# Weight staging, mask, score and ring choices of a planned attention and maxout kernel, five batches split in place of seven

## The chip, the cores and the metric

The kernel runs on one core of a Trainium2 chip. The metric is device time in microseconds of one execution. A core has five engines that run side by side: TensorE (PE: matmuls, with its weight loads shown as PEld), VectorE (DVE), ScalarE (ACT), GpSimd (POOL) and SyncE (SP, which here only issues DMAs and waits for them). Data lie in on-chip memory of 128 partitions; matmuls write to PSUM, a small memory that VectorE and ScalarE read out.

## The reference

Eight batches, eight heads, 576 positions, head size 64. Causal attention with a bias that falls with the running sum of max(s, 0), and then a feed-forward layer whose hidden layer is the largest of three products:

```python
scores = scale * np.matmul(q, k.transpose(0, 1, 3, 2))
cum = np.cumsum(np.maximum(s, 0.0), axis=-1)
bias = -(cum[:, :, :, None] - cum[:, :, None, :])
scores = np.where(causal, -1000000000.0, scores + np.minimum(bias, 0.0))
attn = np.exp(scores - np.max(scores, axis=-1, keepdims=True))
attn = attn / (np.sum(attn, axis=-1, keepdims=True) + 1e-09)
x = np.matmul(attn, v)                      # heads side by side: 4608 x 512
h = np.maximum(np.maximum(x @ w1, x @ w2), x @ w3)   # 768 wide
return h @ w_out
```

All inputs and the output are 32-bit floats, except that the weights arrive as 64-bit floats and are turned on the chip.

## The kernel before

**Splitting numbers.** Most matmuls run in 16 bits: a 32-bit number is kept as a high half and a low half (the rest after rounding), and a product is three matmuls (high by high, high by low, low by high). The scores use 32-bit matmuls: either the raw numbers, or a rounded high part `qh` and a low part `ql` in three terms (`scores_of`, L1125 to L1179). `RAWS` and `RAW0` say which units take raw ones.

**Units.** Two heads share one unit of 128 partitions. `ORDER` lists how batches are worked: `s` (split) does the first 256 rows of queries of a batch, in two units of two head pairs each; `r` (rest) does the other 320 rows of that batch, in four units of one pair; `w` (whole) does both at once, in four units. Before, seven batches are split and one is whole. A unit loads `qr` (q and k), `rv` (v) and `bias` (L744, L753, L857, L868, L880), splits v into `vv` (L808 to L818) and, where scores are not raw, q and k into `qh` and `ql` (L947 to L965). A step of 128 query rows (`one_step`, L1192) is: the causal mask laid over the bias by GpSimd (L1222, for units from `MASKU` on; for units before it TensorE adds a triangle of large negative numbers to the scores, L1159), scores on TensorE (L1149), sum and maximum on VectorE (L1235), exponential on ScalarE (L1244), division into high and low halves (L1280, L1288), a transpose by DMA (L1299), and values on TensorE (L1384, `values`). The last 64 query rows of two units are done together (`both`, L1018). Units 0 and 1 (below `ND`) use 32-bit numbers and TensorE transposes instead (`turned`, L1305).

**Experts.** When all four pairs of a batch's phase (256 or 320 rows) are done, `experts` (L1445) computes the hidden layer, six blocks of three `u` matmul groups (L1479), whose maximum is kept in a tile `m1` (L1494, L1502) and split into halves (L1509 on ScalarE, L1514 on GpSimd, or on VectorE for sets below `EARLYSET`). Then come four `d` groups (L1535), each copied to a tile `o` (L1554) and sent out (L1560). Tiles `m1` come from a ring of three, tiles `o` from a ring of two.

**Weights.** 24 weight blocks (18 for `u`, 6 for the output) are loaded as 64-bit floats (L477), turned into 32-bit floats (`d1` L485 on ScalarE, then either `d2` and `d3` on VectorE, L489 and L493, or `top` on GpSimd, L499, and `join` on VectorE, L506; `LOWP` says for which blocks), scaled per group of three by a bound that TensorE (L527, L434) and VectorE work out, and split into halves (L599, L637). The raw block stays in one of seven places until its halves are made. The first phase of batch 0 does not wait for halves: it uses raw blocks in 32-bit matmuls (`first_set`, L659, L689).

**Bias.** The running sums of all rows are made once (L368 to L399), written to memory and read back for each unit, spread over all partitions. Units below `NPB` do not wait for that: below `NDB` they load their rows of s spread over the partitions and scan them there (L884 to L909); otherwise TensorE spreads the sums with a matmul (L918).

**The order.** Nothing waits in program order by itself. Each operation is handed to a planner (`Plan`) with a cost for each engine that may do it, a key and the tiles that it reads and writes. `Plan.run` (L121) walks through modelled time and lets each free engine take the ready operation with the lowest key; the sequence so found is written out, and every engine then runs its part in that order. So keys (`PACE`, `LOOK`, `FAST`) and costs decide the order of the program, not its work. Operations with a `mode` use TensorE in tiles smaller than its full array; the planner holds one back for a while (`HOLD`, L163) so that several of them go together. DMAs on SP are modelled by `load` (L316):

```python
def load(emit, key, nbytes, reads=(), writes=(), queue="SP", rate=0.3, lat=2000.0, begin=0.0):
    plan.add({queue: (lat, 450.0, nbytes / rate * 1e-3)}, emit, key, reads, writes).ready = begin
```

The functions that the change touches, and what calls them:

## Time and profile before

| | |
|---|---|
| median of three runs | 785.98 us (785.86 to 788.97) |
| the profiled execution | 784.61 us |
| its span, first to last instruction | 782.6 us |
| VectorE, ScalarE, GpSimd busy | 573.8, 519.2, 308.3 us |
| bytes moved by DMA | 136.31 MB |
| `u` matmuls (L1479) | 3240, busy 411.3 us |
| `d` matmuls (L1535) | 1080, busy 137.9 us |

A row of the profile's groups reads: line, engine, operation, written tile <- read tiles, shapes, count | busy us, mean ns of one | idle time of the engine just before them, and what ended most of it. A row of a timeline reads: start us, us, engine, line, operation, tiles, shapes, count, and in brackets the idle time before. A row of waits reads: engine and line <- engine and line waited for: total us, times, longest us. Matmuls overlap each other, so a sum of mean durations is more than the busy time, and the start of one to the start of the next is its price.

### The profile page before, as it was taken

Reading aid. Unit: us, or ns where it says so; the run is one execution under the profiler, and the core shown is the slowest. Engines: PE = TensorE matmul, PEld = TensorE weight load, DVE = VectorE, ACT = ScalarE, POOL = GpSimd, SP = SyncE. Lnnn points to the kernel's source line nnn. Section 1 sums busy time; section 2 is a strip of 40 time slices with the busy share of each in tenths; the row PEclk is TensorE's granted clock in tenths of the full one; section 3 lists DMA queues with packets and bytes.
Section 4 is the critical chain, followed back from the end, with each engine's and each line's share of the span. In section 5 each row is a group of like instructions: output and inputs, shape, how many; then the busy total and the mean of one; then the engine's idle time right before and its main releaser. Section 6 shows DMA issues by size and latency. Waiting matters only on the chain. (4 is left out here: it accounts for less than half of the span.)

```text
span 782.6 us, 19630 instructions
## 1 busy us (share of the span) xinstructions
PE 764.8 (98%) x7189; PEld 589.6 (75%) x7189; DVE 573.8 (73%) x1691; ACT 519.2 (66%) x1369; POOL 308.3 (39%) x361
## 2 busy tenths in 40 slices
PE   7889999999999999999999899999999999999998
PEld 5677888888888877766788677667776777778875
DVE  6999898875587888888878787888787977322131
ACT  6878777871687787986887777777876977111101
POOL 4432423641355455444544364354444452011110
PEclk9999999999999999999999999999999999999999
DMA  9799778890399899998999999898989865300000
GB/s 342 245 260 242 180 169 164 176 237 18 97 207 233 199 175 214 227 215 200 225 232 207 183 192 240 241 190 198 254 210 169 208 137 100 81 1 34 28 2 34
DMA packets 241167, 136.31 MB, mean 174 GB/s; under 512 B 204080, under 2 KB 222000, under 8 KB 241072
## 3 DMA queue, kind: packets, MB, share of 16 engines
q1 hardware_dynamic: 240912, 134.78, 75.7%
q8 instruction: 56, 0.92, 0.5%
q14 instruction: 39, 0.32, 0.2%
q10 hardware_dynamic: 160, 0.30, 0.1%
HBM read 75.64 MB, written 9.58 MB: 109 GB/s over the span
## 5 line engine op out<-in xcount | busy, mean ns | idle before, releaser
L1479 PE MATMUL u<-x,w 128*128 128x320 f16 (+1 forms) x3240 | 411.3, 287 | 2.9 <-ACT o L1554 2.9
L1479 PEld LDWEIGHTS <-w 128*128 128x128 f16 x3240 | 312.6, 98 | 99.5 <-issue 17.6
L1514 POOL TENSOR_TENSOR h<-m,h 128x320 f16<-128x320 f32 (+1 forms) x90 | 69.9, 777 | 190.4 <-ACT h L1509 174.5
L1535 PE MATMUL d<-h,w 128*128 128x320 f16 (+1 forms) x1080 | 137.9, 287 | 0.1
L1502 DVE SCALAR_TENSOR_TENSOR m<-u,m 128x320 f32<-128x320 f32 (+1 forms) x180 | 82.2, 457 | 64.3 <-PE u L1479 60.1
L1535 PEld LDWEIGHTS <-w 128*128 128x128 f16 x1080 | 104.7, 98 | 30.4 <-issue 3.2
L1222 POOL TENSOR_SCALAR_AFFINE_SELECT p<-bias 128x256 f32<-128x256 f32 (+3 forms) x91 | 68.9, 770 | 120.6 <-DVE pr L1288 68.9
L1244 ACT ACTIVATE p<-p,sc 128x256 f32<-128x256 f32 (+3 forms) x182 | 98.2, 540 | 26.3 <-DVE sc L1235 25.6
L1509 ACT ACTIVATE h<-m 128x320 f16<-128x320 f32 (+1 forms) x90 | 39.4, 438 | 102.9 <-DVE m L1502 102.6
L1288 DVE SCALAR_TENSOR_TENSOR pr<-p,sc,pr 128x256 f16<-128x256 f32 (+3 forms) x182 | 100.3, 567 | 8.0 <-ACT pr L1280 7.8
L1280 ACT ACTIVATE pr<-p,sc 128x256 f16<-128x256 f32 (+3 forms) x182 | 89.3, 538 | 13.0 <-DMA pT<-pr 7.9
L961 POOL TENSOR_TENSOR ql<-qr,qh 128x256 fp32r<-128x256 f32 (+1 forms) x76 | 82.5, 1106 | 35.0 <-ACT qh L949 30.6
L1235 DVE CUSTOM_DVE_ANT_0 p<-s,p 128x256 f32<-128x256 f32 (+3 forms) x182 | 80.4, 467 | 3.7 <-POOL p L1222 2.2
L1384 PEld LDWEIGHTS <-vv 128*64 128x64 f16 x1232 | 58.6, 110 | 18.1 <-issue 10.0
L1384 PE MATMUL av<-pT,vv 128*64 128x320 f16 (+3 forms) x1104 | 70.3, 276 | 1.2 <-DVE x L1429 0.8
L1494 DVE TENSOR_SCALAR m<-u 128x320 f32<-128x320 f32 (+1 forms) x55 | 25.3, 461 | 48.2 <-PE u L1479 47.6
L1554 ACT ACTIVATE o<-d,os 128x320 f32<-128x320 f32 (+1 forms) x60 | 28.2, 498 | 47.6 <-PE d L1535 36.8
L766 DVE TENSOR_REDUCE am<-rv 128x1 f32<-128x640 f32 (+1 forms) x44 | 33.9, 777 | 13.2 <-DMA rv<-in_qkv_dram 13.0
L1222 POOL TENSOR_SCALAR_AFFINE_SELECT ha<-bias 128x1024 f32<-128x1024 f32 (+3 forms) x29 | 26.7, 926 | 41.8 <-DVE r L1288 29.8
L1244 ACT ACTIVATE ha<-ha,sc 128x512 f32<-128x512 f32 (+3 forms) x58 | 35.9, 620 | 6.5 <-DVE sc L1235 6.1
L815 DVE SCALAR_TENSOR_TENSOR vv<-rv,vs,vv 128x640 f16<-128x640 f32 (+1 forms) x44 | 39.0, 887 | 0.4
L1288 DVE SCALAR_TENSOR_TENSOR r<-ha,sc,r 128x512 f16<-128x512 f32 (+3 forms) x58 | 37.5, 660 | 2.3 <-ACT r L1280 2.2
(170 smaller groups left out, 980.1 us busy)
## 6 DMA issues: line engine op xcount, KB each, us to landing
bias<-cd SPq DMA_DIRECT2D x32, 576.0 KB, 5.0
qr<-in_qkv_dram SPq DMA_DIRECT2D x28, 480.0 KB, 5.2
rv<-in_qkv_dram SPq DMA_DIRECT2D x32, 320.0 KB, 3.8
raw<-in_w_dram SPq DMA_DIRECT2D x16, 512.0 KB, 5.7
qr<-in_qkv_dram SPq DMA_DIRECT2D x13, 512.0 KB, 6.3
bias<-cd SPq DMA_DIRECT2D x12, 512.0 KB, 5.4
out_dram<-o SPq DMA_DIRECT2D x32, 160.0 KB, 2.4
early<-in_w_dram SPq DMA_DIRECT2D x8, 512.0 KB, 7.0
```

The source lines that it names most:

```text
L961: lambda e, d0=d0, d1=d1: E[e].tensor_tensor(out=lo().bitcast(F32R)[:, d0:d1], in0=raw()[:, d0:d1], in1=hi()[:, d0:d1], op=ALU.subtract),
L1222: nc.gpsimd.affine_select(out=pt()[:, 0:8 * P].rearrange("p (j n) -> p j n", j=2)[:, :, at:at + nk], in_=r["bias"]()[:, 2 * a * w:2 * (a + ...
L1235: lambda e, j=j: nc.vector.tensor_tensor_reduce(out=pj(j), in0=src(j), in1=pj(j) if masked else bias(j), scale=-SCALE, scalar=3.0e38, op0= ...
L1244: lambda e, j=j: nc.scalar.activation(out=pj(j), in_=pj(j), func=AF.Exp, scale=-1.0, bias=nm()[:, j:j + 1], accum_out=sm()[:, j:j + 1]),
L1280: lambda e, h_=h_, s_=s_, j=j: nc.scalar.activation(out=h_(), in_=s_(), func=AF.Copy, scale=ri()[:, j:j + 1]),
L1288: lambda e, h_=h_, l_=l_, s_=s_, j=j: nc.vector.scalar_tensor_tensor(out=l_(), in0=s_(), scalar=ri()[:, j:j + 1], in1=h_(), op0=ALU.mult, ...
L1384: nc.tensor.matmul(av()[j * D:(j + 1) * D, c0:nq], lhsT=lt, rhs=rt, start=(n < 2), stop=(n >= len(todo) - 2), skip_group_check=True,)
L1479: nc.tensor.matmul(pm()[:, :nq], lhsT=v[:, wt, kt, :], rhs=x(xt, kt), start=(k == 0), stop=(k == 3 * NKT - 1),)
L1502: lambda e, pm=pm, m1=m1: nc.vector.scalar_tensor_tensor(out=m1()[:, :nq], in0=pm()[:, :nq], scalar=HSC, in1=m1()[:, :nq], op0=ALU.mult, o ...
L1509: lambda e, m1=m1, ft=ft: nc.scalar.activation(out=h(0, ft), in_=m1()[:, :nq], func=AF.Copy),
L1514: lambda e, m1=m1, ft=ft: E[e].tensor_tensor(out=h(1, ft), in0=m1()[:, :nq], in1=h(0, ft), op=ALU.subtract),
L1535: nc.tensor.matmul(pm()[:, :nq], lhsT=v[:, wt, dt, :], rhs=h(c, ft), start=(k == 0), stop=(k == 3 * NFT - 1), skip_group_check=True,)
```

## The change

It changes constants of the planner and of the kernel, and some functions. In words:

- `ORDER`: batches 0 to 4 are split, 5 to 7 are whole. `RAWS` 10: all split units use raw scores. `MASKU` 4: units 0 to 3 get their mask from TensorE. `NDB` 1: unit 0 scans its own bias. `FUSE0` 2: split units from 2 on compute the values of both pairs in one operation.
- `RAWX`, `RAWAT`: eleven places for raw weight blocks; the four new ones are the two `qh` and two `ql` buffers. `LATE`: the halves get keys later by 10. `PACE`: other weight keys. `LOWP` from 0: blocks 0 and 1 also use GpSimd's `top`.
- Tiles `o` come from the ring of `m1`, now five deep. `EARLYSET` 4: the low halves of expert sets 1 to 3 are made by VectorE. `EARLY` 2: low parts `ql` are always made by GpSimd. `P3` 12: the third set of attention buffers is used from unit 12 on.
- The planner: other rules for grouping operations with a mode, other costs for DMAs (a lead before a transfer occupies the queue, other rates and latencies), for the scale matmul and for the 32-bit transposes; other keys (`LOOK`, `FAST`, `HOLD`).
- New code that its constants leave unused: `far_power` (`FAR` 99), `split_first` (`D16` 0), half PSUM tiles in `first_set` (`KP` 0). The code for the output matmuls moves from `experts` into `down_all` without a change but for the ring and the cost of the load.

```diff
-PACE = (0.9, -1.0, 3000.0)
-EARLY = 8
-EARLYSET = 0
-LOOK = (10.0, 4.0, 5.0, 3.5)
+PACE = (0.5, 3.0, 3000.0)
+EARLY = 2
+EARLYSET = 4
+LOOK = (10.0, 4.0, 2.0, 3.5)
...
-MASKU = 0
+MASKU = 4
...
-FAST = 8
-HOLD = (3000.0, 30000.0)
+FAST = 4
+HOLD = (2000.0, 30000.0, 2)
+SAME = 1
+D16 = 0
+SPARE = 1000.0
+FAR = 99
...
+KP = 0
+HOLD2 = (3000.0, 900.0e3, 2)
...
-NDB = 0
+NDB = 1
...
-RAWS = 6
-FUSE0 = 99
+RAWS = 10
+FUSE0 = 2
...
-P3 = 10
-LOWP = (2, 24)
+P3 = 12
+RAWX = 1
+LATE = 10.0
+LOWP = (0, 24)
...
-ORDER = ('s0', 's1', 's2', 's3', 's4', 's5', 'r0', 'r1', 's6', 'r2', 'r3', 'r4', 'r5', 'r6', 'w7')
+ORDER = ('s0', 's1', 's2', 's3', 's4', 'r0', 'r1', 'r2', 'r3', 'r4', 'w5', 'w6', 'w7')
...
-                    if kept is not None and op.mode:
-                        break
-                    if e == "PE" and op.mode and not shape and op.due > now > HOLD[1]:
-                        kept = op
+                    if e == "PE" and op.mode:
+                        kept.append(op)
+                        if shape and (op.mode == shape or not SAME):
+                            pick = op
+                            break
+                        if not shape and (len(kept) >= (HOLD2 if now > HOLD2[1] else HOLD)[2] or not op.due > now > HOLD[1]):
+                            pick = kept[0]
+                            break
                         continue
-                    pick = op
+                    pick = kept[0] if kept and shape else op
                     break
...
-                    dma[e] = max(dma[e], now + busy) + op.ways[e][2]
+                    dma[e] = max(dma[e], now + op.ways[e][3]) + op.ways[e][2]
...
-        qr=2, qh=2, ql=2, rv=4, vv=2, bias=2, p=2, pr=2, tl=2, pT0=2, pT1=2, tT=2, t=5, m1=3, o=2,
-        sc=6, dg=2, am=3, vs=5, ws=3, os=4, s=2, av=1, m=3,
+        qr=2, qh=2, ql=2, rv=4, vv=2, bias=2, p=2, pr=2, tl=2, pT0=2, pT1=2, tT=2, t=5, m1=5,
+        sc=6, far=1, dg=2, am=3, vs=5, ws=3, os=4, s=2, av=1, m=3,
...
-    def load(emit, key, nbytes, reads=(), writes=(), queue="SP", rate=0.3, lat=2000.0, begin=0.0):
-        plan.add({queue: (lat, 450.0, nbytes / rate * 1e-3)}, emit, key, reads, writes).ready = begin
+    def load(emit, key, nbytes, reads=(), writes=(), queue="SP", rate=0.36, lat=1285.0, begin=0.0, lead=1440.0):
+        plan.add({queue: (lat + SPARE, 400.0, nbytes / rate * 1e-3, lead)}, emit, key, reads, writes).ready = begin
...
-            {"PE": (250.0, 250.0)},
+            {"PE": (250.0, 90.0)},
...
+    RAWAT = [0, 1, 2, 3, 4, 5, RAW, -2, -1, -2, -1, 0, 1, 2, 3, 4, 5, -2, -1, -2, -1, 0, 1, 2]
...
             k = (i if i < RAW else i - 1) % RAW
-            if i == RAW:
+            if RAWX:
+                k = RAWAT[i]
+            if RAWX and i > RAW and k < 0:
+                r = buf("ql" if k == -1 else "qh", name=f"raw{i}")
+            elif i == RAW:
...
-            k = wkey(i)
+            k = wkey(i) + LATE
...
-            o = buf("o", free=True, name=f"o_plain_{dt}")
+            o = buf("m1", free=True, name=f"o_plain_{dt}")
...
-                FIRST, 4 * P * nq, [o], lat=1500.0,
+                FIRST, 4 * P * nq, [o], lat=1320.0, lead=120.0, rate=0.45,
...
-            load(spread, k - LOOK[2], 4 * P * nb_ * rows_, [cd], [bias], lat=4500.0 if u < 4 else 2500.0)
+            load(spread, k - LOOK[2], 4 * P * nb_ * rows_, [cd], [bias], lat=3000.0 if u < 4 else 1065.0, rate=0.266, lead=1590.0)
...
-        tw = lambda n: (2000.0, 1250.0, 200.0 * n)
+        tw = lambda n: (1570.0 + SPARE, 1200.0 if n < 10 else 1450.0 if n < 14 else 2000.0, 156.0 * n, 545.0)
...
-            add({"PE": (350.0 * (qb + 1) + 80.0, 350.0 * (qb + 1))}, turn, t, [(pt, (qb, j)), (pr, (qb, j))], [(m, j)])
+            add({"PE": (270.0 * (qb + 1) + 80.0, 270.0 * (qb + 1))}, turn, t, [(pt, (qb, j)), (pr, (qb, j))], [(m, j)])
...
-            o = buf("o", free=True, name=f"o{n}_{dt}")
+            o = buf("m1", free=True, name=f"o{n}_{dt}")
```

More of the change, by code (lines that the diff above doesn't have):

```diff
@@ L336 @@
     cct = inner("cc", 12 * S, 4 * S)
-    load(lambda e: E[e].dma_start(out=st()[0:HB], in_=s), -1000.0, 4 * HB * S, writes=[st], queue="ACT")
+    load(lambda e: E[e].dma_start(out=st()[0:HB], in_=s), -1000.0, 4 * HB * S, writes=[st], queue="ACT", lat=2000.0)
     def do(e):
@@ L400 @@
     load(
-        lambda e: E[e].dma_start(out=cd(), in_=cct()[0:HB]), -1000.0, 4 * HB * S, [cct], [cd], queue="ACT", lat=5500.0
+        lambda e: E[e].dma_start(out=cd(), in_=cct()[0:HB]), -1000.0, 4 * HB * S, [cct], [cd], queue="ACT", lat=4000.0
     )
@@ L443, in power, with far_power @@
             key, [gm], [(t, 2)],
+        )
+    def far_power(t, key, n):
+        fd = Buf(plan, f"far{n}", lambda b: dram.tile([P, 1], F32, name=f"far{n}"), "one")
+        row = buf("far", name=f"far_row{n}")
+        add(
+            {"DVE": (157.0, 75.0)},
+            lambda e: nc.vector.tensor_scalar(
+                out=t()[:, 1:2], in0=t()[:, 0:1], scalar1=2.0 ** -80, scalar2=1.0 / VSC, op0=ALU.max, op1=ALU.mult
+            ),
+            key, [(t, 0)], [(t, 1)],
+        )
+        load(lambda e: E[e].dma_start(out=fd(), in_=t()[:, 1:2]), key, 4 * P, [(t, 1)], [fd], rate=1.0e-3)
+        load(
+            lambda e: E[e].dma_start(out=row(), in_=fd().rearrange("p o -> o p").to_broadcast([P, P])),
+            key, 4 * P * P, [fd], [row],
+        )
+        add(
+            {"DVE": (282.0, 200.0)},
+            lambda e: nc.vector.tensor_reduce(out=t()[:, 2:3], in_=row(), axis=AX.X, op=ALU.max),
+            key, [row], [(t, 2)],
         )
@@ L642, in weights, with split_first, h @@
         first_set(c, raw)
+    halves_of = {}
+    def split_first(hb):
+        nq = PH[0][1]
+        vs = VS[0, "split"]
+        fac = fixed("fac", [P, 8], F32)
+        add(
+            {"DVE": (145.0, 65.0)},
+            lambda e: nc.vector.tensor_scalar(
+                out=fac()[:, 0:NFT], in0=SWS()[:, 0:NFT], scalar1=vs()[:, 4:5], scalar2=HSC, op0=ALU.mult, op1=ALU.mult
+            ),
+            H16K, [(SWS, i) for i in range(NFT)] + [(vs, 4)], [fac],
+        )
+        h16 = buf("hc", name="h0")
+        def h(c, ft):
+            o = (c * NFT + ft) * nq
+            return h16().bitcast(F16)[:, o:o + nq]
+        for ft in range(NFT):
+            src = lambda ft=ft: hb()[:, ft * nq:(ft + 1) * nq]
+            by = lambda ft=ft: fac()[:, ft:ft + 1]
+            add(
+                {"ACT": act(nq, 200.0)},
+                lambda e, ft=ft, src=src, by=by: nc.scalar.activation(out=h(0, ft), in_=src(), func=AF.Copy, scale=by()),
+                H16K + ft, [(hb, ft), fac], [(h16, (0, ft))],
+            )
+            add(
+                {"DVE": dve(nq)},
+                lambda e, ft=ft, src=src, by=by: nc.vector.scalar_tensor_tensor(
+                    out=h(1, ft), in0=src(), scalar=by(), in1=h(0, ft), op0=ALU.mult, op1=ALU.subtract
+                ),
+                H16K + 0.5 + ft, [(hb, ft), fac, (h16, (0, ft))], [(h16, (1, ft))], True,
+            )
+        down_all(0, 0, nq, h16, h, vs, 1.0e6)
     def first_set(c, raw):
@@ L755, in values_in @@
         sk = (b, kind)
-        if plain(u):
+        if plain(u) and not D16:
             return
@@ L768, in values_in @@
             ),
[L769 removed]
+            AMK if plain(u) else k - 4.0, [rv], [(am, col)],
         )
```

154 lines of the change are left out of this document (90 added, 64 removed).

## The prediction, made before the changed kernel ran

> **What bounds the kernel now.** I read the page first (busy time of each engine), then busy time by stage, then what TensorE waited for, then the timeline of TensorE alone.
>
> ```profile
> span 782.6 us, 19630 instructions
> ...
> PE 764.8 (98%) x7189; PEld 589.6 (75%) x7189; DVE 573.8 (73%) x1691; ACT 519.2 (66%) x1369; POOL 308.3 (39%) x361
> ...
> PEclk9999999999999999999999999999999999999999
> ```
>
> TensorE is busy for 764.8 of 782.6 us, at full granted clock. The profiled execution took 784.61 us, 2.0 us more than its span, and the median of the three runs shown is 785.98, 1.4 us above that. The sum below is made on 784.61; 1.4 is added at its end. What TensorE does not do is 782.6 - 764.8 = 17.8 us: that is all that a better order can win, as long as its work stays the same. Where these 17.8 us lie, by stage (columns: stretch, length, busy PE, PEld, DVE, ACT, POOL, clock, DMA share, GB/s):
>
> ```profile
> 0.00:30.00 30.00, 23.57 (x251) 16.22 (x251) 23.75 (x95) 22.20 (x66) 16.45 (x30) 1.00 0.79 282
> 30.00:76.00 46.00, 43.13 (x440) 35.20 (x439) 44.23 (x164) 39.24 (x116) 12.69 (x19) 1.00 1.07 263
> 76.00:112.00 36.00, 34.82 (x382) 30.37 (x381) 31.60 (x105) 24.13 (x67) 11.49 (x18) 1.00 0.71 175
> 112.00:425.00 313.00, 313.00 (x3050) 250.78 (x3049) 248.19 (x738) 232.31 (x632) 142.94 (x162) 1.00 0.87 189
> 425.00:640.00 215.00, 211.01 (x1909) 151.41 (x1904) 177.48 (x477) 164.49 (x402) 103.38 (x106) 1.00 0.94 207
> 640.00:782.60 142.60, 139.22 (x1172) 105.62 (x1169) 48.51 (x118) 36.83 (x90) 21.30 (x26) 1.00 0.18 41
> ```
>
> TensorE idles 6.4 us in the first 30, 2.9 up to 76, 1.2 up to 112, none up to 425, 4.0 up to 640 and 3.4 after that, nearly all of it the last output's way out. From 30 to 76 us VectorE is busy 44.23 of 46, 96%: there it sets the pace. After 112 it is at 79% and 83%, and TensorE has work in store. The waits of TensorE (total, times, longest), first before 112 us, then after, then the one of ScalarE that stands behind the later ones:
>
> ```profile
> PE m L434 <- DVE ws L425: 3.4, 3, 1.8
> PE m L415 <- DVE identb L361: 1.6, 1, 1.6
> PE u_plain L659 <- PE m L434: 0.9, 1, 0.9
> PE av L1384 <- DVE x L1429: 0.8, 1, 0.8
> ...
> PE m L1324 <- ACT bias L926: 0.7, 1, 0.7
> PE m L434 <- DVE vs L425: 0.6, 1, 0.6
> ...
> PE m L434 <- DVE vs L776: 0.5, 1, 0.5
> ```
> ```profile
> PE u L1479 <- ACT o L1554: 2.9, 2, 2.1
> ```
> ```profile
> ACT o L1554 <- DMA out_dram<-o: 8.8, 6, 3.6
> ```
>
> Early, TensorE stands in its own order behind the small scale matmul (L434), which waits for VectorE's chain of a weight group. Late, 2.9 of the 4.0 us are two stops of the up matmuls behind an output copy, and that copy waited for an earlier output to leave: a ring of two output tiles is too short.
>
> **The change part by part.** Rows for the prices, from TensorE's timeline (start, duration, what):
>
> ```profile
> 35.39 0.93 PE L1149 MATMUL s<-qr 64*128 64x128 f32 x8
> 36.25 2.00 PE L659 MATMUL u_plain<-x,raw 128*128 128x256 f32 x8
> ...
> 88.54 6.72 PE L1479 MATMUL u<-x,w 128*128 128x256 f16 x60
> 95.10 0.60 PE L689 MATMUL d_plain<-h_plain,early 128*128 128x256 f32 x2
> ```
> ```profile
> 140.20 0.49 PE L1149 MATMUL s<-qr 64*128 64x128 f32 x4
> 140.44 0.37 PE L1149 MATMUL s<-qh 64*128 64x256 f32 x2
> 140.64 0.28 PE L1149 MATMUL s<-qh,ql 64*128 64x256 f32 x2
> 140.76 0.28 PE L1149 MATMUL s<-ql,qh 64*128 64x256 f32 x2
> 140.98 1.48 PE L1479 MATMUL u<-x,w 128*128 128x256 f16 x12
> 142.39 0.69 PE L1384 MATMUL av<-pT,vv 128*64 128x256 f16 x12
> ...
> 180.65 0.22 PE L434 MATMUL m<-identb,vs 128*128 128x128 bf16 x1
> 180.70 1.47 PE L1479 MATMUL u<-x,w 128*128 128x256 f16 x12
> ```
>
> *Raw scores in all split units (RAWS 10, five split batches).* Counted from the two orders, 20 instead of 12 score operations of a split or whole pair use raw float32 and 12 instead of 20 use high and low parts. The raw one takes 36.25 - 35.39 = 0.86 us, the other 140.98 - 140.20 = 0.78. 8 x 0.08 = **+0.6 us** on TensorE (0 to 1.4). In exchange the split units lose their high parts on ScalarE and low parts on VectorE or GpSimd, and two batches are no longer loaded twice. After 112 us those engines are not the bound, so this counts nothing; without that cover it would be a gain.
>
> *Causal mask on TensorE for units 0 to 3 (MASKU 4).* 8 score operations get four 128-column matmuls each. The nearest row is L434 of the same shape, 180.70 - 180.65 = 0.05 us apart, say 0.06: 32 x 0.06 = 1.9. Each masked operation also leaves and enters row tiles once more. A visit to tiles costs 0.1 on the way in (12 up matmuls take 142.39 - 140.98 = 1.41 us before one, where 60 without one take 6.56, so 12 take 1.31) and, I estimate, as much on the way back: 8 x 0.2 = 1.6. Sum 3.5. All lie in the first 50 us, where TensorE idles anyway; half of the operations fall in the first 15 us, so I take half, **+1.7** (0 to 3.5).
> The Trainium skill, "TensorEngine Tiling (Array Packing)", section "Key Properties", says that changing the tiling mode drains TensorE; it names no price and speaks against this edit. The trace agrees, with the 0.10 us above; without a drain this sum would be 0.8 lower.
>
> *Unit 0's bias by a broadcast load and scans on VectorE (NDB 1), low bits of weights 0 and 1 on GpSimd (LOWP).* VectorE's rows of the first 112 us, and the load that is nearest to the new one:
>
> ```profile
> L489 DVE TENSOR_SCALAR early<-early 128x512 int32<-128x512 int32 x2 | 0.9, 466 | 0.0
> ...
> L375 DVE TENSOR_TENSOR_SCAN early<-early 64x256 f32<-64x256 f32 x1 | 0.7, 676 | 0.0
> ```
> ```profile
> L918 PE MATMUL m<-early 64*128 64x256 f32 x16 | 3.8, 381 | 0.6 <-DVE early L385 0.6
> ```
> ```profile
> bias<-cd SPq DMA_DIRECT2D x12, 512.0 KB, 5.4
> ```
>
> Four scans of 0.68 and four scalings (estimate 0.2 each) are +3.5 on VectorE, and L489 takes 0.9 with it: +2.6 in the first 15 us, where its 6.2 us of idle time (30 - 23.75) mostly lie before the first data. TensorE loses half of L918, 1.9 us of work, two bias copies and the 0.7 us wait on one, and the first softmax no longer waits for GpSimd's mask. I take **+1.0 - 0.7 = +0.3** (-2 to +3.5); the start is VectorE's chain, so the 1.9 are not counted. The new load is issued on ScalarE's queue, where only the table load stands behind it.
> The Trainium skill, "DMA: Bandwidth & Descriptors", section "Issuing engines are not separate DMA queues", says that a second issuing engine saves only issue time: the 512 KB would share the DMA engines with the first loads. By that the start is later by 512 KB at the 282 GB/s of the first row above, an estimate of 1.9 us, and the sum is 1.9 higher; no run here shows it yet.
>
> *Values of both pairs in one operation (FUSE0 2), fewer batches split.* From the two orders, value operations of the first phase fall from 32 to 24. Eight visits to tiles at 0.1 to 0.2: **-1.2** (0 to -1.6). HOLD waits 2 us instead of 3 for a partner, which can undo some.
>
> *One ring of five for outputs and maxima.* The 2.9 us of the late waits go. Next late would be an output whose transfer takes more than five openings of the ring, some 2.4 to 3.3 us against more than 10 us of matmuls. **-2.9** (0 to -4.0).
>
> *Eleven raw places, halves later (RAWX, PACE, LATE).* Weight 7 and later ones no longer wait for an earlier weight's halves, so the plain up matmuls can run on while VectorE still owes the halves. What this touches are the waits listed before 112 us behind L434, ws, vs and x: 3.4 + 0.9 + 0.8 + 0.6 + 0.5 = 6.2. The places lent by the high and low parts' buffers are wanted back only by the first rest units, after the split ones. VectorE's total up to 76 us stays, so I take a bit over half, **-3.5** (0 to -6.2).
>
> *Low halves of sets 1 to 3 on VectorE (EARLYSET 4).* On GpSimd one takes 0.75 us, and a VectorE operation of this size 0.42:
>
> ```profile
> L1514 POOL TENSOR_TENSOR h<-m,h 128x256 f16<-128x256 f32 x4 | 3.0, 749 | 8.2 <-ACT h L1509 6.2 <-ACT sc L1252 2.0
> ```
> ```profile
> L1502 DVE SCALAR_TENSOR_TENSOR m<-u,m 128x256 f32<-128x256 f32 x9 | 3.7, 416 | 2.5 <-PE u L1479 1.3 <-ACT pr L1280 1.2
> ```
>
> 18 x 0.42 = 7.5 us more for VectorE, spread over some 90 us in which TensorE has work in store: **0** (0 to +2.5, a third of it, if set 1 runs while VectorE is still full). *Other keys and transfer prices* only reorder; **0** (-2 to +2), since no row prices them.
>
> Sum: +0.6 + 1.7 + 0.3 - 1.2 - 2.9 - 3.5 = **-5.0**. 784.6 - 5.0 = 779.6, and 1.4 to the median: **781.0 us**.
>
> **The rivals.** (0.5%, 3.9 us, is about what a measurement of this kernel can tell from no change: the lines are 782.1 and 789.9.)
>
> *The early gaps only move.* VectorE has the same work up to 76 us, and at 96% its order can change which matmul stands, not how long. Then only the ring and the fused values count: -2.9 - 1.2 + 0.6 + 1.7 + 0.3 = -1.5, 784.5 us. For it: 44.23 of 46. Against it: the 3.4 us behind ws are order, not load. The same band takes in the forecast with a late start: the 512 KB of bias among the first loads are 1.9 us at the 282 GB/s of the first stage, 782.9. Chance 0.31, with all that ends between 782.1 and 789.9.
>
> *VectorE is overfilled (slower).* Before 76 us it gets the 2.6 us of bias work and, if the first expert set begins there, the 2.5 us of EARLYSET; its idle time from 30 to 76 is 46 - 44.23 = 1.8. If halves come ahead of attention after all and the masks stay on the path (3.5), the start slips by 2.6 + 2.5 + 3.5 = 8.6, less the ring's 2.9, plus raw scores 0.6: +6.3, 792.3 us. It decides from the point at which the plain down matmuls end later than 112 us by more than 3. Chance 0.14.
>
> *All gaps close.* Early waits -6.2, ring -4.0, fused -1.6, start -2, masks hidden, raw 0.6: -13.2, 772.8 us. It needs VectorE to be no bound at all. Chance 0.05.
>
> **How the numbers follow.** Forecast 0.50, own range 775.5 to 782.1; rivals 0.31, 0.14 and 0.05. Faster is 0.50 + 0.05 = 0.55, the same 0.31, slower 0.14. The range 775.5 to 790.5 leaves out the third rival (0.05) and nearly all of the slower one (0.13); its upper end also holds the sum with the upper ends of masks, bias and raw scores (+1.8 + 3.2 + 0.8 on 781.0 gives 786.8) and EARLYSET (789.3).
>
> **What would show it.** Right: no wait of an output copy for an output's transfer, and no up matmul behind such a copy; TensorE's idle time from 30 to 112 us under 2 us; plain up matmuls in longer runs, starting near 30 us; TensorE busy within 2 us of 764.8. Wrong: plain up matmuls that start after 33 us (bias or load at the start); waits behind L434 as long as before; a new wait of VectorE's maxima for a transfer, which would mean that the common ring ties TensorE to the output queue; or TensorE's busy time changed by more than 3 us, which would mean that visits to tiles were priced wrongly.

## The result, and the profile after

The changed kernel takes 795.04 us (median of four executions, 793.0 to 797.57), the one before 785.92 beside it. The ratio is 1.0108, 95% interval 1.0069 to 1.0146: slower by 1.1%, some 8.5 us. The prediction was 781.0 us, range 775.5 to 790.5. It was wrong in sign and outside its range.

The profiled execution is the slowest of the four, 797.57 us. The page of after, the same parts as were shown of before (span; busy time, share and instructions by engine; granted clock in 40 slices):

```profile
span 795.8 us, 19558 instructions
...
PE 775.3 (97%) x7195; PEld 592.8 (74%) x7195; DVE 569.0 (72%) x1687; ACT 511.6 (64%) x1361; POOL 274.9 (35%) x317
...
PEclk8999999999999999999999999999999999999999
```

The span is 13.2 us longer. TensorE is busy for 10.5 us more (775.3 against 764.8) and idle for 2.7 us more (20.5 against 17.8). VectorE, ScalarE and GpSimd all do less than before. In the row of clocks only the first digit differs, an 8 in place of a 9. Busy time by stage (columns as before):

```profile
0.00:30.00 30.00, 25.55 (x181) 16.36 (x183) 20.51 (x82) 17.86 (x57) 11.35 (x22) 0.83 0.98 349
30.00:76.00 46.00, 45.30 (x475) 36.22 (x472) 44.61 (x176) 41.09 (x120) 9.62 (x14) 1.00 0.83 223
76.00:112.00 36.00, 36.00 (x422) 30.65 (x420) 33.34 (x120) 23.29 (x75) 8.43 (x14) 1.00 0.80 191
112.00:425.00 313.00, 303.02 (x2825) 232.00 (x2825) 248.99 (x680) 227.91 (x569) 127.79 (x136) 0.99 0.87 192
425.00:640.00 215.00, 212.86 (x2027) 156.71 (x2024) 178.08 (x532) 173.73 (x477) 99.15 (x108) 1.00 0.87 184
640.00:795.80 155.80, 152.53 (x1280) 120.87 (x1274) 43.51 (x104) 27.75 (x67) 18.61 (x25) 1.00 0.15 35
```

Set TensorE's idle time (length less busy) beside that of before. First 30 us: 4.4 (6.4 before). To 76: 0.7 (2.9). To 112: none (1.2). From 425 to 640: 2.1 (4.0). After 640: 3.3 (3.4). So 7.3 us of gaps closed up to 640 us, where the prediction had looked for 6.4 (staging 3.5, ring 2.9); some of the early ones closed because TensorE was slower there. But from 112 to 425 us, where TensorE never stood before, it now stands for 10.0 us, and the first 30 us run at a mean granted clock of 0.83. These two are the result. What TensorE waited for (total, times, longest), below it the group of the scale matmuls for `vs` in after and in before, then VectorE's wait for v, and last the same wait in the kernel before:

```profile
PE m L448 <- DMA bias<-cd: 4.6, 1, 4.6
PE m L448 <- DVE vs L439: 4.5, 5, 1.4
PE s L1250 <- issue: 2.3, 1, 2.3
...
PE m L448 <- DVE ws L439: 0.6, 2, 0.4
```
```profile
L448 PE MATMUL m<-identb,vs 128*128 128x128 bf16 x12 | 2.8, 231 | 9.1 <-DMA bias<-cd 4.6 <-DVE vs L439 4.5
```
```profile
L434 PE MATMUL m<-identb,vs 128*128 128x128 bf16 x14 | 3.1, 223 | 1.2 <-DVE vs L425 1.0 <-ACT o L1554 0.3
```
```profile
DVE am L864 <- DMA rv<-in_qkv_dram: 19.3, 15, 3.1
```
```profile
DVE am L766 <- DMA rv<-in_qkv_dram: 13.0, 13, 2.4
```

L448 is the small scale matmul that was L434 before. Behind a weight group's `ws` it waited 3.4 us, now 0.6. Behind a phase's `vs` (the bound of v, from the maxima of the loaded `rv`) it now waits 9.1 us, where it waited 1.2, and VectorE's maxima wait 19.3 us for v instead of 13.0. The wait of an output copy for an earlier output, 8.8 us before, is no longer in ScalarE's list.

**The stop at 394 us.** The timeline around it, rows of SP, VectorE and TensorE (start, duration, engine, line; brackets: idle before):

```profile
388.50 1.93 SPq L1400 DMA_TRANSPOSE pT<-pr  x1
390.48 0.57 SPq L851 DMA_DIRECT2D rv<-in_qkv_dram  x1
390.68 3.46 PE L1627 MATMUL u<-x,w 128*128 128x320 f16 x24
...
391.14 3.83 SPq L1400 DMA_TRANSPOSE pT<-pr  x1
395.01 0.82 DVE L864 TENSOR_REDUCE am<-rv 128x1 f32<-128x640 f32 x1 [1.19 <-DMA rv<-in_qkv_dram]
...
398.49 0.15 DVE L439 TENSOR_SCALAR vs<-vs 128x1 bf16<-128x1 f32 x1
...
398.69 0.29 PE L448 MATMUL m<-identb,vs 128*128 128x128 bf16 x1 [4.56 <-DMA bias<-cd]
398.91 2.98 PE L1485 MATMUL av<-pT,vv 128*64 128x320 f16 x24
```

The load of `rv` shown is the second of two; it left SP only after a transpose that held SP for 1.93 us, and landed near 395.0. Its maximum, four softmax operations of 0.75 us and two tiny ones followed. The four softmax operations, which VectorE's own order put ahead of the bound, are some 2.5 of the 4.56 us; the late load is the rest. L448 stood first in TensorE's order the whole time, and the 24 value matmuls behind it ran at once when it was through; how long they had been ready the rows do not say. The profile names a bias transfer as the releaser; by the rows it was the chain rv, am, vs. With two more stops of this kind (1.4 us at 286, 1.0 at 339) and two of up matmuls (1.4 and 0.6) that is 9.0 of the 10.0.

**The clock at the start.** After in stretches of 5 us, and TensorE's timeline:

```profile
10.00:15.00 5.00, 2.72 (x14) 1.33 (x13) 4.88 (x23) 3.41 (x13) 2.09 (x3) 0.75 1.02 409
15.00:20.00 5.00, 5.00 (x24) 3.58 (x23) 3.88 (x15) 4.18 (x16) 3.57 (x5) 0.50 1.07 381
20.00:25.00 5.00, 4.90 (x74) 4.01 (x75) 3.33 (x17) 3.72 (x13) 0.89 (x2) 0.72 1.05 393
```
```profile
12.63 0.80 PE L1250 MATMUL s<-qr 64*128 64x128 f32 x4 [2.28 <-issue]
...
28.26 0.49 PE L1250 MATMUL s<-qr 64*128 64x128 f32 x4
28.69 0.29 PE L1261 MATMUL s<-tri,identb 128*128 128x128 bf16 x2
28.90 0.70 PE L1250 MATMUL s<-qr 64*128 64x256 f32 x4
29.54 0.28 PE L1261 MATMUL s<-tri,identb 128*128 128x128 bf16 x2
29.75 0.87 PE L1485 MATMUL av<-pT,rv 128*64 128x256 f32 x8
...
41.29 0.49 PE L1250 MATMUL s<-qr 64*128 64x128 f32 x4
...
42.68 3.68 PE L743 MATMUL u_plain<-x,raw 128*128 128x256 f32 x16
```

TensorE stands 2.28 us before 12.63, and from then on the same four matmuls take 0.80 us that take 0.49 at 28.26. By the trace's clock records the half clock lasted from 12.5 to 22.8 us, 10.24 us, and once more 3.41 us from 398.2, near the end of the 4.56 us stop: 13.65 us at half speed, which lengthens busy time by up to 6.8 us. The masks add to it as well. A masked score operation is two score parts, each followed by two mask matmuls. It takes 29.75 - 28.26 = 1.49 us where a raw one takes 0.86, 0.63 more, if matmuls on tiles follow, and 42.68 - 41.29 = 1.39, 0.53 more, if matmuls on the full array follow. Four of the eight are of each kind: 4.6 us in all at full clock. The two sums are 11.4, a little more than the 10.5 that TensorE's busy time grew; other edits take work away, such as half of the matmuls that spread the bias.

Why TensorE stood at 10.4: unit 0's softmax began late, because its bias load took 8.3 us from issue to landing (first row below, of the DMA issues; the nearest row of before had 5.4), and the third score operation needs a PSUM tile that this softmax frees.

```profile
bias<-in_s_dram ACTq DMA_DIRECT2D x1, 512.0 KB, 8.3
```
```profile
9.77 0.50 DVE L999 TENSOR_SCALAR bias<-bias 128x256 f32<-128x256 f32 x2 [2.40 <-DMA bias<-in_s_dram]
10.18 1.26 DVE L1006 TENSOR_TENSOR_SCAN bias<-bias 128x256 f32<-128x256 f32 x2
11.36 0.26 DVE L1336 CUSTOM_DVE_ANT_0 p-4_254<-s-4_209,bias 128x128 f32<-128x128 f32 x1
```

The first softmax operation starts at 11.36; before, it started at 9.23. This profile is an extreme in that: in the other runs below that keep this load, it took 6.9 to 7.9 us to land, and where the masks stay on TensorE the first softmax started at 9.93 to 10.87.

### The profile page after: what moved, and what is told of

Its sections match the earlier page's. It is cut to its first block, busy times and chain, and to the rows that moved or that the text cites. A ratio compares the mean times of both kernels' runs of the same rounds, so it can differ in the third digit from the quotient of the medians.

```text
span 795.8 us, 19558 instructions
## 1 busy us (share of the span) xinstructions
PE 775.3 (97%) x7195; PEld 592.8 (74%) x7195; DVE 569.0 (72%) x1687; ACT 511.6 (64%) x1361; POOL 274.9 (35%) x317
## 4 chain that ended last, share of the span: by engine, by line
PE 44%; DVE 4%; DMA 3%; issue 1%; POOL 1%; ACT 0%; SPq 0%; DVEq 0%; POOLq 0%; ACTq 0%
PE u L1627 25%; PE d L1564 10%; PE av L1485 4%; PE s L1250 3%; DMA rv<-in_qkv_dram 1%; DMA bias<-cd 1%; PE s L1131 1%; DVE p L1336 1%; DVE pr L1389 1%; DVE m L1650 1%; DMA pT<-pr 0%; DVE am L864 0%; DVE r L1389 0%; DVE vv L916 0%; DVE ha L1336 0%
## 5 line engine op out<-in xcount | busy, mean ns | idle before, releaser
L1662 POOL TENSOR_TENSOR h<-m,h 128x320 f16<-128x320 f32 (+1 forms) x72 | 56.2, 781 | 183.3 <-ACT h L1657 172.8
L1345 ACT ACTIVATE p<-p,sc 128x128 f32<-128x128 f32 (+3 forms) x192 | 104.0, 543 | 15.9 <-DVE sc L1336 15.6
L1389 DVE SCALAR_TENSOR_TENSOR pr<-p,sc,pr 128x128 f16<-128x128 f32 (+3 forms) x184 | 104.5, 580 | 7.9 <-ACT pr L1381 7.8
L1381 ACT ACTIVATE pr<-p,sc 128x128 f16<-128x128 f32 (+3 forms) x184 | 91.0, 546 | 22.5 <-DVE sc L1363 11.7
L1062 POOL TENSOR_TENSOR ql<-qr,qh 128x256 fp32r<-128x256 f32 (+1 forms) x64 | 70.7, 1124 | 42.2 <-ACT qh L1050 36.1
L1336 DVE CUSTOM_DVE_ANT_0 p<-s,p 128x512 f32<-128x512 f32 (+3 forms) x168 | 77.6, 489 | 4.2 <-POOL p L1323 3.4
L864 DVE TENSOR_REDUCE am<-rv 128x1 f32<-128x640 f32 (+1 forms) x40 | 31.4, 786 | 19.3 <-DMA rv<-in_qkv_dram 19.3
L1389 DVE SCALAR_TENSOR_TENSOR r<-ha,sc,r 128x384 f16<-128x384 f32 (+3 forms) x56 | 36.7, 664 | 3.5 <-ACT r L1381 3.3
L1323 POOL TENSOR_SCALAR_AFFINE_SELECT ha<-bias 128x768 f32<-128x768 f32 (+3 forms) x28 | 23.4, 842 | 42.9 <-DVE r L1389 25.8
L1381 ACT ACTIVATE r<-ha,sc 128x384 f16<-128x384 f32 (+3 forms) x56 | 30.6, 596 | 10.7 <-DVE sc L1363 5.3
L1050 ACT ACTIVATE qh<-qr 128x896 fp32r<-128x896 f32 (+1 forms) x32 | 31.3, 981 | 9.2 <-DMA qr<-in_qkv_dram 8.1
```

The costliest lines, as they stand in the source:

```text
L1062: lambda e, d0=d0, d1=d1: E[e].tensor_tensor(out=lo().bitcast(F32R)[:, d0:d1], in0=raw()[:, d0:d1], in1=hi()[:, d0:d1], op=ALU.subtract),
L1323: nc.gpsimd.affine_select(out=pt()[:, 0:8 * P].rearrange("p (j n) -> p j n", j=2)[:, :, at:at + nk], in_=r["bias"]()[:, 2 * a * w:2 * (a + ...
L1336: lambda e, j=j: nc.vector.tensor_tensor_reduce(out=pj(j), in0=src(j), in1=pj(j) if masked else bias(j), scale=-SCALE, scalar=3.0e38, op0= ...
L1345: lambda e, j=j: nc.scalar.activation(out=pj(j), in_=pj(j), func=AF.Exp, scale=-1.0, bias=nm()[:, j:j + 1], accum_out=sm()[:, j:j + 1]),
L1381: lambda e, h_=h_, s_=s_, j=j: nc.scalar.activation(out=h_(), in_=s_(), func=AF.Copy, scale=ri()[:, j:j + 1]),
L1389: lambda e, h_=h_, l_=l_, s_=s_, j=j: nc.vector.scalar_tensor_tensor(out=l_(), in0=s_(), scalar=ri()[:, j:j + 1], in1=h_(), op0=ALU.mult, ...
```

## The experiments

Each time stands beside runs of the kernel before on the same chip (its medians there were 786.1 to 787.4), so kernels are compared by their ratio to it; 0.1% is 0.8 us. Most intervals are about ±0.2%, so a difference of two such ratios is good to about ±0.3%, 2.3 us. "After" stands at 1.0108 with ±0.4%, from four executions, so a difference from it is good to about 3.4 us. What is read from a profile (idle time, waits) is one execution of each kernel.

### What is it: the start, the order of batches, or the prices?

**Fill the stop at the start.** Ten throw-away matmuls of 512 columns ahead of unit 1's second bias matmul, in the same order otherwise; they write a tile that is overwritten.

```diff
+                    for _ in range(10 if i == 2 else 0):
+                        nc.tensor.matmul(m(), lhsT=identb(), rhs=..., start=True, stop=True)
```

> The changed kernel with ten extra 512-column matmuls of the identity (about 2.1 us at full clock) ahead of the second bias matmul of unit 1, in the stretch from 10.4 to 12.6 us in which TensorE stood; their result is overwritten. The order of everything else is the same. Theory A (the 2.3 us stop at 10.4 us is what puts TensorE at half clock from 12.5 to 22.8 us, and that delays the start): the clock stays at 1.0 there and the time falls by 2 to 5 us from 795, to 790 to 793. Theory B (the start is VectorE's chain, which the clock does not touch): clock at 1.0, time within 1 us of 795.

Measured: 795.01 us, 1.0100 [1.0064, 1.0137]. The half clock was not avoided, it came later (6.8 us from 16.8, after another stop of 1.49 us). Nothing follows for the time: this run is inconclusive.

**The order of before (seven split batches) in the changed kernel.**

```diff
-ORDER = ('s0', 's1', 's2', 's3', 's4', 'r0', 'r1', 'r2', 'r3', 'r4', 'w5', 'w6', 'w7')
+ORDER = ('s0', 's1', 's2', 's3', 's4', 's5', 'r0', 'r1', 's6', 'r2', 'r3', 'r4', 'r5', 'r6', 'w7')
-RAWS = 10
+RAWS = 12
```

> The changed kernel with the order of before: seven batches split, one whole (raw scores for the first six split batches). Theory A (five split batches leave TensorE too few expert sets in store, so that it stands at each batch's scale matmul from 263 to 580 us): the idle time from 112 to 640 us falls from 12.1 us to under 5 and the time by 6 to 9 us, to 786 to 789. Theory B (the stops come from the other keys and transfer prices): the idle time stays over 9 us and the time within 3 us of 795.

Measured: 803.01 us, 1.0212 [1.0176, 1.0248]. TensorE's two largest waits there:

```profile
PE m L448 <- DVE vs L439: 9.3, 6, 2.9
PE u L1627 <- DVE m L1650: 6.7, 5, 2.8
```

(`RAWS` 12 makes six of the seven split batches raw.) The theory that the five split batches cost the time fell: with seven it is 1.0% slower still, and the scale matmul stands as long. The stops do not come from the order of batches.

**The start of before: no masks on TensorE, no bias load for unit 0.**

```diff
-MASKU = 4
+MASKU = 0
-NDB = 1
+NDB = 0
```

> The changed kernel with the mask on GpSimd for all units and unit 0's bias from TensorE, as before. Theory A (these two edits set the late first softmax at 11.4 us in place of 9.2, the half clock after it, and 3.5 us of TensorE work): no half clock before 30 us, eight visits to tiles fewer, and 4 to 7 us less, 788 to 791. Theory B (they are hidden at the start): within 2 us of 795.

Measured: 797.95 us, 1.0134 [1.0101, 1.0166], no faster than after. Neither theory foresaw this: the timeline of TensorE shows a new stop at the start and a long half clock that begins within it (13.7 us from 12.4):

```profile
10.30 0.93 PE L1250 MATMUL s<-qr 64*128 64x128 f32 x8
16.76 1.65 PE L1250 MATMUL s<-qr 64*128 64x128 f32 x8 [5.53 <-DVE sc L1336]
```

The edit was exchanged for another accident of the plan: ScalarE stood behind the issue of the table `cd` (at 13.71 us) and unit 1's bias copy was queued after it. With the changed kernel's prices this pair of switches says nothing of its own cost.

**All prices of transfers as before.** The planner's lead, rate and latency for loads, outputs and transposes go back; no other line changes. (Two of the edited places are shown; those of the outputs, the bias loads, the table `cd` and two other transposes are left out.)

```diff
-    def load(..., rate=0.36, lat=1285.0, begin=0.0, lead=1440.0):
-        plan.add({queue: (lat + SPARE, 400.0, nbytes / rate * 1e-3, lead)}, ...)
+    def load(..., rate=0.3, lat=2000.0, begin=0.0, lead=450.0):
+        plan.add({queue: (lat, 450.0, nbytes / rate * 1e-3, 450.0)}, ...)
-        tw = lambda n: (1570.0 + SPARE, 1200.0 if n < 10 else 1450.0 if n < 14 else 2000.0, 156.0 * n, 545.0)
+        tw = lambda n: (2000.0, 1250.0, 200.0 * n, 1250.0)
```

> The changed kernel with the transfer prices of before (rates, latencies and no lead) in its planner; all else as changed. Theory A (too few expert sets in store): the stops at the batches' scale matmuls from 112 to 640 us stay, 9 us or more, and the time is within 4 us of 795. Theory B (the new prices let v arrive too late, so that the scale matmul stands in TensorE's order ahead of work that was ready): the idle time from 112 to 640 us falls below 6 us and the time by 5 to 9.

Measured: 787.86 us, 1.0008 [0.9989, 1.0028]: 1.0% less than after, 7.9 us. The stage where TensorE stood, and its wait for `vs`:

```profile
112.00:425.00 313.00, 310.51 (x2947) 238.57 (x2944) 254.91 (x695) 232.18 (x584) 128.88 (x139) 1.00 0.87 197
```
```profile
PE m L448 <- DVE vs L439: 2.0, 3, 1.0
```

Idle 2.5 us instead of 10.0, scale matmul 2.0 instead of 9.1. VectorE's wait for `rv` falls from 19.3 to 8.5 us. The two kernels compute the same and TensorE has the same 7195 matmuls; the edit is to numbers in the planner alone, which change the order and give some operations to another engine (VectorE 1701 instead of 1687, ScalarE 1346 instead of 1361). This is most of the loss.

### Which prices, and through what?

**Loads and outputs alone:** of the prices above, those of `load` and of the tables and outputs go back, those of the transposes stay. (One of the places is shown.)

```diff
-    def load(..., rate=0.36, lat=1285.0, begin=0.0, lead=1440.0):
+    def load(..., rate=0.3, lat=2000.0, begin=0.0, lead=450.0):
```

> The changed kernel with only the prices of its loads and stores set back (rate, latency, no lead, no spare); the prices of the transposes stay as changed. Theory A (the loads' new price lets q, k, bias and v be asked for too late): time falls to 787 to 790 as with all prices set back, and the scale matmuls' stops from 112 to 640 us shrink under 6 us. Theory B (it is the transposes' price, which crowds the queue): within 3 us of 795.

Measured: 795.92 us, 1.0117 [1.0092, 1.0143], no better than after. VectorE waits 19.3 us for `rv`, as in after.

**Transposes alone:** the other half of the same edit, one of its three places shown.

```diff
-        tw = lambda n: (1570.0 + SPARE, 1200.0 if n < 10 else 1450.0 if n < 14 else 2000.0, 156.0 * n, 545.0)
+        tw = lambda n: (2000.0, 1250.0, 200.0 * n, 1250.0)
```

> The changed kernel with only the prices of the DMA transposes set back; loads and stores keep the new prices. Theory A (the transposes' price is the cause, since setting back the loads alone left 795.9): 786 to 790, idle time of TensorE from 112 to 640 us under 5 us in place of 12.1. Theory B (the two sets of prices only fit together): 793 or more, idle time there 8 us or more.

Measured: 789.47 us, 1.0059 [1.0037, 1.0081], 3.9 us less than after, just clear of the noise. From 112 to 425 us TensorE is idle for 2.6 us, as with all prices back, and VectorE waits 14.8 us for `rv`.

**Of the transposes only what the queue is charged**, 545 to 1250 ns ahead of a transfer and 156 to 200 ns a block; landing and SP's own price stay as changed.

```diff
-        tw = lambda n: (1570.0 + SPARE, ..., 156.0 * n, 545.0)
+        tw = lambda n: (1570.0 + SPARE, ..., 200.0 * n, 1250.0)
```

> The changed kernel with only two of the numbers in the transposes' price set back: 1250 ns of lead in place of 545 and 200 ns a block in place of 156, so that the plan's queue is occupied longer by each; its latency and issue time stay as changed. Theory A (the occupied queue is what the new price understates): 788 to 791. Theory B (the end of a transpose, not the queue, counts): within 2 us of 795.

Measured: 788.59 us, 1.0020 [1.0001, 1.0038], 6.9 us less than after. Yet the scale matmul still stands:

```profile
PE m L448 <- DVE vs L439: 6.0, 3, 2.4
```

TensorE's idle time in all fell from 20.5 to 14.4 us, of which the scale matmul gave 3; the stops of up matmuls and part of the one at the start went too. VectorE waits 13.3 us for `rv`. So the queue's charge is enough to win most of it back, but not by one wait alone. The new price is not far off in the middle: for a transpose of eight blocks on a free queue it gives 0.545 + 8 x 0.156 + 1.57 + 1.0 (`SPARE`) = 4.36 us to landing, the old one 1.25 + 8 x 0.2 + 2.0 = 4.85, and in the trace of after the transposes of L1400 (all sizes) land after 4.3 in the median. But they range from 2.4 to 9.4 us, and the cheaper price leaves less room for the late ones; that this is why it loses was not tested by itself.

**Slack for the chain in front of the scale matmul.** All prices stay as changed; the planner is told that the first small VectorE operation of a phase's `vs` takes 3 us longer to arrive, so it puts L448 later in TensorE's order. What is computed stays the same.

```diff
-    def power(t, key):
+    def power(t, key, slack=0.0):
...
-        add({"DVE": (157.0, 75.0)}, do, key, [(t, 0)], [(t, 1)])
+        add({"DVE": (157.0 + slack, 75.0)}, do, key, [(t, 0)], [(t, 1)])
...
-                power(vs, kk)
+                power(vs, kk, 3000.0)
```

> The changed kernel, with 3 us added to what the planner takes as the delay of the first of VectorE's small operations between the maxima over v and the scale matmul, so that this matmul is put later in TensorE's order. Theory A (TensorE stands at this matmul while work behind it is ready, since v's loads come later than the plan has them): idle time from 112 to 640 us falls from 12.1 to under 7, time to 789 to 792. Theory B (when it stands there nothing else is ready, since the attention as a whole lags the plan): the stops move to other matmuls, idle time stays over 9 us, time within 2 us of 795.

Measured: 789.57 us, 1.0038 [1.0014, 1.0061], 5.5 us less. The waits of TensorE, largest first:

```profile
PE u L1627 <- DVE m L1650: 2.0, 3, 0.8
...
PE av L1485 <- DMA pT<-pr: 1.6, 2, 0.9
PE av L1485 <- ACT vv L911: 1.5, 1, 1.5
```

L448 is gone from the list. Part of its time came back: value matmuls wait 3.4 us (0.5 in after), up matmuls behind `m` 2.0 (1.1). TensorE's idle time from 112 to 640 us falls from 12.1 to 6.0. The prices are those of after, so this shows the mechanism: an engine that works in a written order stood at a matmul that the plan had put too early.

### The start, with the old prices underneath

**No masks on TensorE**, all prices as before.

```diff
-MASKU = 4
+MASKU = 0
```

> The changed kernel with the transfer prices of before and the mask of all units on GpSimd. Theory A (a masked score operation costs TensorE 1.49 in place of 0.86 us, 8 x 0.63 = 5.0 in all, and none of it is hidden): TensorE's busy time falls by 4 to 6 us from 773.2 and the time from 787.9 to 782 to 785. Theory B (all of it lies in the start, where VectorE is the chain): busy time falls, idle time rises by as much, time within 1.5 us of 787.9.

Measured: 786.95 us, 1.0010 [0.9989, 1.0031], against 1.0008 with the masks: no difference. TensorE's busy time falls by 6.1 us (773.2 to 767.1) and its idle time grows by 7.5 (12.1 to 19.6); from 0 to 30 us it is busy for 21.70 us instead of 25.20. The masks' work lies in time that TensorE would have idled. Not all of the 6.1 is masks: half clock lasted 10.2 us at the start with them and 6.8 without.

**No bias load for unit 0**, masks kept, all prices as before.

```diff
-NDB = 1
+NDB = 0
```

> The changed kernel with the transfer prices of before and unit 0's bias from TensorE; the masks of units 0 to 3 stay on TensorE. Theory A (unit 0's broadcast load is what delays the first softmax, by 2 us, and what brings the half clock): no half clock before 30 us, 783 to 785.5 against 787.9. Theory B (it takes the masks away as well): within 1.5 us of 787.9.

Measured: 784.38 us, 0.9980 [0.9957, 1.0002], 2.2 us less than with the load, about as much as the noise. Here, in stretches of 5 us as above, is the time that ran at half clock in after:

```profile
10.00:15.00 5.00, 5.00 (x42) 3.81 (x40) 3.91 (x21) 5.00 (x22) 3.09 (x6) 1.00 1.03 399
15.00:20.00 5.00, 4.62 (x40) 3.38 (x38) 4.84 (x20) 4.41 (x14) 3.52 (x5) 1.00 1.06 395
```

The clock is full, the first softmax starts at 9.06.

**Neither masks nor bias load:** both of these edits together.

> The changed kernel with the transfer prices of before, the mask of all units on GpSimd and unit 0's bias from TensorE. Theory A (the broadcast load of unit 0's bias delays the first softmax by 2 us and puts TensorE at half clock; without it the clock stays at 1.0): 780 to 784. Theory B (the new weight keys delay the start just as well): half clock for some 7 to 14 us again, 786 or more.

Measured: 783.50 us, 0.9973 [0.9949, 0.9997], 2.9 us less than without the masks alone. The two estimates for the load agree, 2 to 3 us; each alone is little more than the noise, their mean, 2.5, is good to 1.7. This pair also gives the masks at full clock: without them TensorE is busy for 768.0 us, with them (the run above) 772.0, so 4.0, and the times differ by 0.6 us, within the noise.

**What half clock alone costs at the start.** One warm-up matmul in place of eight; all else, the order too, is the kernel without the bias load.

```diff
-            for i in range(WARM):
+            for i in range(1):
```

> The kernel of 784.4 us with one warm-up matmul in place of eight; its order is the same, and so is all other work. It measures the half clock at the start by itself. Theory A (TensorE's clock in the first 25 us is worth some us, so the half clock explains much of the 3.5 us that unit 0's load costs): half clock until 10 us or longer, time 786 to 788. Theory B (VectorE's chain sets the start, so the late first softmax is the price): half clock, but within 1 us of 784.4.

Measured: 789.38 us, 1.0032 [1.0012, 1.0051], 0.52% more: 4.1 us. The same score matmuls and masks, early and a little later:

```profile
15.35 1.22 PE L1250 MATMUL s<-qr 64*128 64x256 f32 x4
16.50 0.40 PE L1261 MATMUL s<-tri,identb 128*128 128x128 bf16 x2
...
19.28 0.28 PE L1261 MATMUL s<-tri,identb 128*128 128x128 bf16 x2
19.49 0.70 PE L1250 MATMUL s<-qr 64*128 64x256 f32 x4
```

TensorE ran at about half speed up to some 18 us. So slow matmuls at the start do lengthen the whole kernel, here by 4.1 us, no less than all that the bias load costs. What part of the load's 2 to 3 us is the half clock and what part the late softmax itself was not separated; the fill above was meant to.

### The other parts

**Staging as before** (seven places, halves early), on the kernel with old prices and the old start.

```diff
-RAWX = 1
-LATE = 10.0
-PACE = (0.5, 3.0, 3000.0)
+RAWX = 0
+LATE = 0.0
+PACE = (0.9, -1.0, 3000.0)
```

> The kernel of 783.5 us (changed kernel with the transfer prices, masks and unit 0's bias of before) with the weights staged as before too: seven raw places, halves not later, old weight keys. Theory A (eleven places and later halves are worth something: the idle time from 30 to 112 us is 2.5 us here and was 4.1 before): 785.5 to 788. Theory B (VectorE's load sets that stretch whatever the order): within 1.5 us of 783.5.

Measured: 788.19 us, 1.0037 [1.0020, 1.0054], 5.0 us more than with the new staging. The way there is not the one predicted: TensorE waits for `ws` 0.2 us here and 1.6 with the new staging. Its idle time from 30 to 112 us is 3.8 against 2.5, and in the whole run 19.0 against 16.4. Where the rest of the 5.0 lies is not shown.

**Seven split batches**, on the same kernel: the edit of `ORDER` and `RAWS` shown above.

> The kernel of 783.5 us (changed kernel with the transfer prices, masks and unit 0's bias of before) with seven batches split as before. Theory A (seven split batches keep more expert sets in store; idle time from 112 to 640 us is 4.3 us here): 780 to 782.5. Theory B (each split batch costs more loads and halves than the store is worth, as the 803 us under the new prices say): 785 to 790.

Measured: 786.64 us, 1.0014 [0.9994, 1.0034], 3.2 us more than with five. Fused values and raw scores stay in this run, so it tests the number of split batches alone.

**The ring of five alone, in the kernel before.**

```diff
-t=5, m1=3, o=2,
+t=5, m1=5,
-            o = buf("o", free=True, ...)
+            o = buf("m1", free=True, ...)
```

> The kernel before with one ring of five for outputs and maxima in place of three and two; nothing else is changed. Theory A (the ring's two stops are its price): the waits of output copies for an output's transfer go from 8.8 us to under 1, the 2.9 us of up matmuls behind them go, and the time falls by 2 to 4 us against the kernel before. Theory B (the order is reshuffled and new stops take their place): within 1.5 us of before.

Measured: 788.27 us, 1.0024 [1.0006, 1.0041]: 1.9 us more than before, no gain. The wait for outputs is gone, but the list of TensorE's waits now begins like this:

```profile
PE m L434 <- DVE vs L425: 4.4, 6, 1.7
```

The wait for `vs` grew from 1.0 to 4.4 us: stops moved from output copies to scale matmuls, and TensorE's idle time stays (18.0 us of the span, 17.8 before).

### A version that beats both

**The changed kernel with the old prices, without the bias load, with 3 us of slack:** the three edits shown above together.

> The same 3 us in the kernel of 784.4 us (changed kernel with the transfer prices of before and unit 0's bias from TensorE). Theory A: its idle time of 5.5 us from 112 to 640 falls below 3.5, time 782 to 783. Theory B: within 1.5 us of 784.4.

Measured: 781.31 us, 0.9941 [0.9915, 0.9967]: 0.6% faster than before, 0.39% faster than without the slack. Its page, and the group of the scale matmuls for `vs` (busy, mean ns, idle before):

```profile
span 779.5 us, 19562 instructions
...
PE 770.8 (99%) x7203; PEld 590.7 (76%) x7203; DVE 568.8 (73%) x1695; ACT 508.3 (65%) x1347; POOL 277.9 (36%) x317
```
```profile
L448 PE MATMUL m<-identb,vs 128*128 128x128 bf16 x12 | 2.7, 223 | 0.0
```

TensorE idles 8.7 us in all, half of what it did before, and none of it at a scale matmul for `vs`; it is busy for 6.0 us more, of which the masks are 4.0 to 4.6.

## Why the prediction was wrong, step by step

- *Other keys and transfer prices only reorder: 0 (-2 to +2).* **The step that failed.** It measured +7.9 us, four times its bound. "Since no row prices them" held for the work, not for the time: the waits of VectorE showed 13.0 us behind `rv` before, on the queue that the transposes use, and the step did not ask what a plan with cheaper transposes would put ahead of `rv`, and what stands behind its chain on TensorE. The runs showed instead that TensorE stands 9.1 us at the scale matmul, most of it in a stage where it had never stood. The transposes' prices are 3.9 to 6.9 us of the loss, and 3 us of slack at that matmul alone win 5.5 back. That edits of the same prices give 3.9, 6.9 and 7.9 suggests that each new plan throws some 2 to 3 us of stops anew; it is not clear of the noise. The other keys (`LOOK`, `FAST`, `HOLD`) were not tried.
- *Unit 0's bias: +0.3 (-2 to +3.5).* Measured +2 to 3, near the upper end. The count of VectorE's work was beside the point (20.5 of 30 us busy, less than the 23.75 of before). In the profile of after the load took 8.3 us to land, the first softmax came 2.1 us later, and after a 2.28 us stop TensorE ran at half clock; in the other runs with the load and the masks the softmax came 0.7 to 1.6 us later. The Trainium skill, "DMA: Bandwidth & Descriptors", section "Issuing engines are not separate DMA queues", had the right sign: 1.9 us by the estimate from it, 0.7 to 2.1 measured to the first softmax. That a stop costs clock as well was in no step.
- *Masks: 3.5 on TensorE, 1.7 counted.* By the rows 4.6, by busy time 4.0 where the clock was full, so somewhat too little: the step put a masked operation at 0.24 + 0.2 = 0.44 us, the rows have 0.53 to 0.63. In time it was -0.2 and +0.6, both ± 2.3. That it would be hidden was right, and more so than counted.
- *Eleven raw places: -3.5.* The size is right, 5.0 ± 2.3 us, the reason is not shown. The wait for `ws` fell from 3.4 to 0.6 between before and after, but with the old staging put back it is 0.2, and idle time from 30 to 112 us differs by only 1.2. That the size fits is partly luck.
- *Raw scores and fused values of five split batches: +0.6 - 1.2.* Not tested by themselves. Five split batches in place of seven, with raw scores and fused values in both, are worth -3.2 ± 2.5 with the old prices and -8.2 ± 4.1 with the new ones (1.0108 against 1.0212); the loads and halves saved, which the step put at nothing, may be part of that.
- *One ring: -2.9.* The wait vanished as told; the time did not follow. "Next late would be an output whose transfer takes more than five openings of the ring" was wrong: next late was the scale matmul.
- *The slower rival.* Its marker fired: the plain up matmuls start at 37.6 us (33 was the line) and the last plain down matmul ends at 117.4 (115 was the line). Its mechanism did not: VectorE is as full from 30 to 76 us as before (44.61 of 46, 44.23 before), but TensorE stands for only 0.7 us from 30 to 112. Two of the four signs of being right came true too: no output copy waits for an output's transfer any more, and that 0.7 is under 2. And the busy time changed by 10.5 us, which was to mean that visits to tiles were priced wrongly; up to 6.8 of it was the clock. A marker that other causes can also trip proves little.
- *"The early gaps only move".* This rival (0.31) came nearest in kind, but it moved gaps among the first 76 us. The early gaps did close; new ones came in a later stage that had had none, and with the old transfer prices most of these are gone too (2.5 us from 112 to 425).

The parts do not add up to the whole. Old prices and old start leave 0.9973, 2.1 us less than before, though staging (5.0) and five split batches (3.2) are worth 8.2 there. The other 6 us must lie in edits that were not taken back: the ring, the rules for grouping, `FUSE0` and raw scores, `LOWP`, `EARLY`, `EARLYSET`, `P3`, `LOOK`, `FAST`, `HOLD` and the costs of the scale matmul and the 32-bit transposes, or in the plans' own scatter. Of those only the ring was tried alone, in the kernel before (+1.9); the rest is open.

## What to carry to other kernels

A planner's price is an edit like any other: where an engine works in a written order, a price that leaves too little room on a shared queue can make it stand at a small operation that depends on that queue. So list the bound engine's short operations that wait for another engine, and give them slack: here 3 us on one operation won 5.5 us with the new prices and 3.1 with the old ones. And when a wait is removed, ask what the same engine would wait for next in each later stage, also in those where it now never waits; and read the granted clock of the first stage before pricing any stop there.

## What the hardware did that was not expected

- The granted clock went to half at the end of a stop of 2.28 us, with TensorE busy before and after, and it took 10.24 us to come back. In the records of the runs here half-clock stretches last about 3.4, 6.8, 10.2 or 13.7 us. The Trainium skill, "TensorE: Matmul & The Clock Gate", section "What's actually happening", describes a free-running window of 3413 ns; the lengths agree with it. The Trainium skill, the same page, section "HAM oscillation — how this bites in real kernels", states that idle gaps above some 3.4 us are to be avoided; here half clock began within or less than 1 us after shorter ones (2.28 us in after, 1.49 in the run with filler, 1.08 in the run with only the queue's charge set back), while others brought none (2.1 us at 443 in before). Where in the window a stop falls may decide; that was not tested.
- With one warm-up matmul the trace has no clock record before 18 us and the profile shows 1.00 there, though the rows above show matmuls at half speed. In the other runs too the records begin only at 4.3 to 7.2 us. The duration of a known matmul is the better witness.
- A masked score operation costs 0.53 us more than a raw one if matmuls on the full array follow, 0.63 if matmuls on tiles follow. The difference, 0.10, is one more change of the array's shape, the price that the prediction had. The 0.53 holds two such changes beyond the raw operation's one; what is left makes a mask matmul 0.08 us, where the prediction took 0.06 from a matmul among others of its shape.
